# Seven half-size products for the last quarter of one token group's first matrix product, and a new order of work around it

## The chip, the cores and the metric

The kernel runs on one NeuronCore of a Trainium2 chip. Its engines are TensorE (PE, with PEld for its weight loads), VectorE (DVE), ScalarE (ACT), GpSimd (POOL) and SyncE (SP, which here only issues DMAs). The metric is the time of one execution on the device in microseconds. Before the change it is 272.64 us, the median of three runs (272.38 to 273.44).

## What is computed

Linear attention with cosine weights for 8 batches of 8 heads, 576 positions and 64 features, followed by a two-layer network on the 4608 tokens that come out:

```python
r = np.maximum(x, 0.0)                      # x is q or k
phi = np.concatenate([r * cos, r * sin], axis=-1)
kv = np.einsum('bhsf,bhsd->bhfd', k_p, v)
z = np.sum(k_p, axis=2)
num = np.einsum('bhsf,bhfd->bhsd', q_p, kv)
den = np.einsum('bhsf,bhf->bhs', q_p, z)[..., None] + 1e-06
x = (num / den).transpose(0, 2, 1, 3).reshape(4608, 512)
h = x @ w_in                                # 512 x 2048
g = np.maximum(0.01 * h, h)
out = g @ w_out                             # 2048 x 512
```

Inputs and output are float32; the matmuls take float16 and accumulate in float32.

## The kernel before

**Groups.** The tokens are worked in nine groups, numbered 0 to 8, of 512: group b below 8 holds the first 512 positions of batch b, group 8 the last 64 positions of all eight. "Third group" is group 2 and "fourth group" group 3. Each group goes through the same stages: k and v are loaded, k is multiplied with cosine and sine (`k_cos(b,j,engine)`, `k_sin`, nine slices j each, tile `kp`), v is cast (`v_pairs`, tile `vm`), `kv_sum(b)` multiplies them (72 matmuls); q is loaded, multiplied (`q_prep(g,j)`, tile `qp`) and transposed by DMA (`q_transpose_dma`, tile `qpT`); `num(g,j)` makes 128 tokens' numerators and denominators in the one PSUM buffer `ps_num`, and three DVE operations (`den`, `rden`, `xs`) divide them; the four `xs` are transposed, from group 3 on by one DMA (`x_transpose_dma(g)`, tile `xT`). `load(k,b)` and its like issue on SP's queue into four `stage` buffers, so that a load waits until its buffer's last tenant has been read.

**First product.** In groups 0 to 2 `M(g,m)` makes 128 of the 2048 columns of h for all 512 tokens with four matmuls of 512 columns (L634), and ACT applies the leaky ReLU to two m at once (L645, tile `g`). From group 3 on (`F7 = 3`) a quarter u of the columns is made by seven half-size products in Winograd's form: `P(g,u,n)`, n = 1 to 7, is four matmuls of 256 columns (L787). They need sums of quarters of x (`x_sum(g,n,engine)`: X1, X2, X4, and n = 3, which overwrites a quarter of `xT`) and of the weights (`w1_sum(bp,n,engine)`: W1, W2, W4 in `wext`, and n = 3, which overwrites a quarter of the weights). The products of one quarter share three of four PSUM banks `ps_f`, and `e(g,u,letter)` combines them: b copies the first bank to the third, s copies the second to `s5`, u copies the third to `u1`, z and y are DVE additions, and a, c, d, e are leaky ReLUs from PSUM to `g` on ACT (L814). b, s and u run on ACT, with capital letters on DVE. So P6 waits for b, P3 for s, P7 for u, P4 for y, and the next quarter's P5 for a.

**Second product.** From group 1 on it is made by seven half-size products for the whole group: `F(g,i)`, i = 0 to 27, is four matmuls of 256 columns (L904); `g_sum` makes the sums of g on DVE.

**Order.** Nothing is scheduled at run time: a table of operations (`PROGRAM`, 1,126 entries) is walked from the top, and every operation appends its instructions to its engine's queue. Each engine works its own queue in that order and waits on semaphores. The line order of the table is thus the order in each engine's queue, and the engine letter at an operation's end (D, A, P) says whose queue it is.

The lines that the change touches stand below; in `w1_sum` and `x_sum`, `need` is an assertion at build time that an operation has already been recorded, and issues nothing.

Of the kernel before, what the change touches and what calls it, by code (L numbers as in the profile page):

```python
# [54 lines left out]
F(1,13) k_cos(3,1,P) F(1,14) k_sin(3,8,P) k_cos(3,4,A) k_sin(3,3,D) k_cos(3,8,P) F(1,15) v_pairs(3,2,4,P)
q_transpose_dma(3,0) k_cos(3,7,A) q_prep(3,3,0,8,A) k_cos(3,6,D) num(2,2) x_transpose(2,1,A) k_sin(3,7,D)
k_sin(3,2,D) F(1,16) F(1,17) F(1,18) num(2,3) q_transpose_dma(3,1) k_sin(3,1,A) k_sin(3,6,A) F(1,19)
x_transpose(2,2,A) F(1,20) F(1,21) F(1,22) v_pairs(3,0,2,A) x_transpose(2,3,A) F(1,23) kv_sum(3,0,4,n) M(2,0)
load(v,4) w1_sum(0,1,D) M(2,1) num(3,0) M(2,2) M(2,3) w1_sum(1,1,D) num(3,1) load(k,4) M(2,4) M(2,5) M(2,6)
# [10 lines left out]
kv_sum(4,0,4,n) P(3,1,3) F(2,9) P(3,1,7) e(3,1,z) e(3,0,c) e(3,1,e) num(4,0) F(2,10) w1_sum(1,3,D) F(2,11)  # L70
P(3,2,1) F(2,12) P(3,2,5) e(3,2,b) k_cos(5,6,A) e(3,1,y) num(4,1) P(3,2,6) k_cos(5,3,D) P(3,1,4) k_sin(5,1,P)
e(3,2,s) k_sin(5,6,P) k_cos(5,4,P) q_prep(5,0,0,8,P) P(3,2,2) F(2,13) k_sin(5,2,D) num(4,3) F(2,14) P(3,2,3)
e(3,1,c) e(3,2,u) e(3,2,z) e(3,2,a) load(q,6) P(3,2,7) e(3,1,d) e(3,2,y) k_sin(5,5,A) k_cos(5,2,A)
q_prep(5,2,0,8,P) F(2,16) e(3,2,e) k_cos(5,8,A) P(3,3,1) num(4,2) q_prep(5,3,0,8,D) F(2,15) P(3,3,5)
k_cos(5,5,P) q_prep(5,1,0,8,D) F(2,17) e(3,3,b) x_transpose_dma(4) q_transpose_dma(5,0) v_pairs(5,2,4,A)
P(3,3,6) F(2,18) P(3,3,2) g_sum(2,4,0,4) e(3,3,s) e(3,3,u) k_cos(5,7,A) P(3,2,4) e(3,2,c) P(3,3,3)
x_sum(4,1,P) F(2,19) g_sum(2,4,4,8) F(2,20) k_sin(5,4,P) k_cos(5,0,A) v_pairs(5,0,2,A) P(3,3,7) e(3,3,a)
k_sin(5,0,P) e(3,3,y) e(3,3,c) F(2,21) e(3,2,d) F(2,22) e(3,3,z) e(3,3,e) F(2,23) F(2,24) F(2,25) F(2,26)
F(2,27) P(3,3,4) e(3,3,d) P(4,0,1) e(4,0,b) F(3,0) x_sum(4,2,D) P(4,0,5) F(3,1) load(k,6) e(4,0,s) P(4,0,2)
P(4,0,6) F(3,2) x_sum(4,3,D) k_cos(5,1,A) P(4,0,3) k_sin(5,8,A) e(4,0,u) e(4,0,a) g_sum(3,1,4,8,2) P(4,0,7)  # L80
k_sin(5,3,A) k_sin(5,7,P) e(4,0,z) F(3,3) g_sum(3,2,4,8,2) P(4,1,1) g_sum(3,1,0,4,1) e(4,0,e) e(4,0,y)
e(4,1,b) P(4,1,5) g_sum(3,2,0,4,1) kv_sum(5,0,4,n) e(4,1,S) P(4,1,2) e(4,1,a) q_transpose_dma(5,1) P(4,1,6)
e(4,0,c) F(3,4) x_sum(4,4,D) g_sum(3,3,5,8,2) q_prep(6,0,0,8,P) load(v,6) num(5,0) F(3,5) P(4,0,4) e(4,1,u)
P(4,1,3) e(4,0,d) k_cos(6,2,A) P(4,1,7) P(4,2,5) g_sum(3,3,0,4,1) e(4,1,z) k_sin(6,6,P) g_sum(3,3,4,8,2)
# [10 lines left out]
P(5,0,1) e(5,0,b) P(5,0,5) e(5,0,s) F(4,0) P(5,1,1) x_sum(5,2,P) P(5,0,2) q_prep(7,0,0,8,A) F(4,1)
g_sum(4,3,5,8,2) F(4,2) e(5,0,a) g_sum(4,2,0,4,1) x_sum(5,4,D) P(5,0,3) num(6,0) P(5,0,6) e(5,0,u) e(5,0,z)
F(4,3) F(4,4) P(5,0,7) e(5,0,e) e(5,0,y) F(4,5) e(5,1,b) P(5,1,5) e(5,1,s) q_prep(7,2,0,8,D) num(6,1) P(5,0,4)
F(4,6) e(5,0,d) g_sum(4,3,0,4,1) P(5,1,2) e(5,0,c) q_prep(7,1,0,8,P) P(5,1,6) F(4,7) e(5,1,a) P(5,1,3)
e(5,1,u) e(5,1,z) load(v,7) e(5,1,e) P(5,2,1) P(5,1,7) F(4,8) e(5,1,y) e(5,2,b) F(4,9) num(6,2) F(4,10)
# [1125 lines left out]
```

## Time and profile before

| | |
|---|---|
| median of the runs | 272.64 us (272.38 to 273.44) |
| the profiled execution | 272.81 us, its span 271.0 us |
| PE | busy 263.6 us, 97% |
| PEld, DVE, ACT, POOL | 81%, 76%, 66%, 48% |
| granted TensorE clock | 1.0 |

The span runs from the first instruction to the last, and 1.8 us of the execution lie around it. The trace gives for each engine its instructions with their start and duration, and for idle time what ended it. A matmul's duration runs past the start of the next one, as matmuls are pipelined; what a matmul costs is the distance from start to start. For the same reason a row on DVE or ACT may begin a little ahead of the end of the row before.

### The profile page before, as it was taken

How to read it: one execution, taken by the hardware profiler on the slowest of the kernel's cores; microseconds unless marked ns; L12 is line 12 of the kernel's file. 1: busy time of each engine (PE TensorE's matmuls, PEld its weight loads, DVE VectorE, ACT ScalarE, POOL GpSimd, SP SyncE). 2: the span in 40 equal slices, each digit the busy share in tenths (PEclk: the TensorE clock that was granted, in tenths of full speed). 3: DMA queues.
4: the chain of work that ended last, by engine and by line, in shares of the span. 5: the costliest groups of instructions: out<-in, count | busy, mean ns of one | idle time of the engine just before them, and what ended most of it. 6: DMA issues, size and time to landing. Idle time of an engine off the chain costs nothing.

```text
span 271.0 us, 7060 instructions
## 1 busy us (share of the span) xinstructions
PE 263.6 (97%) x2877; PEld 218.5 (81%) x2877; DVE 206.6 (76%) x419; ACT 178.8 (66%) x311; POOL 129.3 (48%) x104
## 2 busy tenths in 40 slices
PE   7899999999999999999999999999999999999993
PEld 3575455656975599999999999999999899999983
DVE  4850597778977897997989689997789967757852
ACT  7856548478966878898788786776834564565500
POOL 2586001992889276979992879743230004000000
PEclk9999999999999999999999999999999999999999
DMA  6999999999999899789959993893565052111214
GB/s 234 359 396 414 379 398 372 373 310 245 293 199 312 182 219 367 239 138 292 300 98 199 252 374 100 141 204 86 120 155 119 2 116 79 41 41 39 80 39 117
DMA packets 75041, 57.07 MB, mean 211 GB/s; under 512 B 47233, under 2 KB 63617, under 8 KB 74625
## 3 DMA queue, kind: packets, MB, share of 16 engines
q1 hardware_dynamic: 74400, 56.11, 74.4%
q10 hardware_dynamic: 608, 0.52, 0.6%
q8 instruction: 22, 0.36, 0.5%
q14 instruction: 11, 0.08, 0.1%
HBM read 36.70 MB, written 9.44 MB: 170 GB/s over the span
## 4 chain that ended last, share of the span: by engine, by line
PE 92%; DMA 3%; POOL 1%; SPq 1%; DVE 1%; issue 0%
PE ps L904 35%; PE ps_f L787 27%; PE ps_h L634 15%; PE ps_o L661 5%; DMA kst<-in_k_dram 3%; PE ps_num L560 3%; PE ps_kv L473 3%; PE ps_f L904 1%; POOL kp L398 1%; PE ps_kv L1004 1%; PE ps_xT L1077 1%; PE ps_qt L546 1%; PE ps_numh L1055 1%; SPq L274 0%; SPq L260 0%; PE ps_x L536 0%
## 5 line engine op out<-in xcount | busy, mean ns | idle before, releaser
L904 PEld LDWEIGHTS <-g 128*128 128x128 f16 x640 | 61.8, 98 | 6.8
L904 PE MATMUL ps<-w,g 128*128 128x256 f16 x496 | 65.1, 273 | 0.0
L814 ACT ACTIVATE g<-ps_f 128x512 f16<-128x512 f32 x72 | 42.0, 598 | 19.1 <-PE ps_f L787 9.7
L634 PE MATMUL ps_h<-xT,w 128*128 128x512 f16 (+1 forms) x208 | 43.5, 363 | 0.0
L787 PEld LDWEIGHTS <-w 128*128 128x128 f16 x384 | 41.6, 114 | 0.7
L787 PE MATMUL ps_f<-xT,w 128*128 128x256 f16 x288 | 42.1, 273 | 0.0
L634 PEld LDWEIGHTS <-w 128*128 128x128 f16 x208 | 22.7, 114 | 16.2
L398 POOL TENSOR_SCALAR kp<-kst,cos_t 128x256 f16<-128x256 f32 (+1 forms) x23 | 30.4, 1328 | 5.0 <-DMA kst<-in_k_dram 5.0
L645 ACT ACTIVATE g<-ps_h 128x1024 f16<-128x1024 f32 x24 | 24.1, 1024 | 12.7 <-PE ps_h L634 12.7
L904 PE MATMUL ps<-T,ext 128*128 128x256 f16 x240 | 32.2, 273 | 0.0
L787 PEld LDWEIGHTS <-wext 128*128 128x128 f16 x288 | 31.3, 114 | 0.6
L904 PEld LDWEIGHTS <-ext 128*128 128x128 f16 x256 | 24.9, 98 | 2.5
L398 POOL TENSOR_SCALAR qp<-qst,cos_t 128x512 f16<-128x512 f32 (+1 forms) x10 | 19.5, 1946 | 9.0 <-DMA qst<-in_q_dram 5.4
L787 PE MATMUL ps_f<-X,wext 128*128 128x256 f16 x144 | 21.5, 273 | 0.0
L687 DVE TENSOR_TENSOR osb<-ps,ext 128x512 f32<-128x512 f32 x23 | 15.8, 687 | 6.4 <-PE ps L904 5.9
L687 DVE TENSOR_TENSOR ps_f<-ps_f,u 128x512 f32<-128x512 f32 x24 | 16.6, 693 | 5.0 <-PE ps_f L787 3.1
L576 DVE TENSOR_TENSOR xs<-ps_num,rden 128x512 f16<-128x512 f32 x28 | 19.4, 691 | 1.0
L398 POOL TENSOR_SCALAR kp<-kst,sin_t 128x256 f16<-128x256 f32 x15 | 18.7, 1249 | 2.3 <-PE ps_kv L473 2.3
L814 ACT ACTIVATE g<-y 128x512 f16<-128x512 f32 x24 | 15.2, 632 | 6.7 <-DVE y L687 6.6
L398 POOL TENSOR_SCALAR qp<-qst,sin_t 128x512 f16<-128x512 f32 (+1 forms) x10 | 19.4, 1942 | 0.0
L687 DVE TENSOR_TENSOR ext<-g 128x512 f16<-128x512 f16 (+1 forms) x24 | 13.9, 578 | 5.1 <-ACT g L645 3.5
L687 DVE TENSOR_TENSOR y<-ps_f,s 128x512 f32<-128x512 f32 x24 | 16.4, 683 | 1.4 <-PE ps_f L787 1.3
(122 smaller groups left out, 457.6 us busy)
## 6 DMA issues: line engine op xcount, KB each, us to landing
out_dram<-osb SPq DMA_DIRECT2D x32, 256.0 KB, 2.9
qst<-in_q_dram SPq DMA_DIRECT2D x7, 1024.0 KB, 9.4
kst<-in_k_dram SPq DMA_DIRECT2D x5, 1152.0 KB, 7.6
vst<-in_v_dram SPq DMA_DIRECT2D x5, 1152.0 KB, 9.8
w2st<-in_moe_w_out_dram SPq DMA_DIRECT2D x3, 1024.0 KB, 12.8
vst<-in_v_dram SPq DMA_DIRECT2D x4, 576.0 KB, 6.7
ext<-in_moe_w_in_dram SPq DMA_DIRECT2D x4, 512.0 KB, 10.5
kst<-in_k_dram SPq DMA_DIRECT2D x2, 576.0 KB, 7.7
```

Of the source, the lines that this page charges most:

```text
L398: eng.tensor_scalar(out=o, in0=i, scalar1=0.0, scalar2=col, op0=ALU.max, op1=ALU.mult)
L473: nc.tensor.matmul(ps[:, o, (c - lo) * NE : (c - lo + 1) * NE], lhsT=st["kp", b][sl, c, j, :], rhs=vm[sl, c, j, :], start=(j == 0), stop=( ...
L546: nc.tensor.transpose(ps[:, h, :], qp[:, h, :], ident)
L560: nc.tensor.matmul(ps[lo:hi, h // 4, (h % 4) * NE : (h % 4 + 1) * NE], lhsT=qpT[:, h, lo:hi], rhs=kv[b][:, h, :],)
L576: nc.vector.tensor_tensor(out=xs, in0=ps[:, :, 0 : 4 * NE].rearrange("p a (b e) -> p a b e", e=NE)[:, :, :, 0:D], in1=rden.rearrange("p (a ...
L634: nc.tensor.matmul(ps[:, m % 2, lo:hi], lhsT=w1[m // 4, c][0][:, w1[m // 4, c][1], m % 4 : 512 : 4], rhs=xT[:, lo // P : hi // P, c, :], s ...
L645: nc.scalar.activation(st["g", g][:, m - 1 : m + 1, :], ps, AF.Lrelu)
L661: nc.tensor.matmul(st["ps_o", g, tt], lhsT=st["g", g][:, m, tt * P : (tt + 1) * P], rhs=w2[:, m, :], start=(m == 0), stop=(m == NFT - 1),)
L687: eng.tensor_tensor(out=o, in0=a, in1=b, op=op)
L787: nc.tensor.matmul(ps[:, mi * HT : (mi + 1) * HT], lhsT=a[:, c, 2 * r0 + mi : 512 : 4], rhs=b[:, c], start=(n in (1, 5) and mi == 0 and c ...
L814: nc.scalar.activation(st["g", g][:, m : m + 2, r * HT : (r + 1) * HT], {"a": A, "c": y22, "e": E, "d": B_}[e].rearrange("p (m t) -> p m t ...
L904: nc.tensor.matmul(ps[:, tt], lhsT=a[:, i, tt * P : (tt + 1) * P], rhs=b[:, i], start=(first and i == 4 * halves[0]), stop=(i == NPR - 1 a ...
```

## The change

A constant `MIX = (3,)` is new: quarter u = 3 of group 2 (m = 10, 11, 14 and 15) is now made by P(2,3,1) to P(2,3,7) and e(2,3,...) in the place of M(2,10), M(2,11), M(2,14) and M(2,15). This brings x_sum(2,1) to x_sum(2,4), asks that all of the weight sums of the second half, W(1,1) to W(1,4), stand before it, and moves the third sum of x (which overwrites a quarter of group 2's `xT`) behind the twelve remaining M(2,m). In the code only the assertions differ:

```diff
+    MIX = (3,)
...
         if n == 3:
-            need(*(("f1", F7 - 1, 8 * bp + 4 + i) for i in range(4)))
+            need(*(("f1", F7 - 1 - (2 * bp + i // 2 in MIX), 8 * bp + 4 + i) for i in range(4)))
...
     def x_sum(g, n, eng):
...
-        if g > F7 and n in (2, 4):
+        if g == F7 - 1 and n == 3:
+            need(*(("f1", g, m) for m in range(NFT) if 2 * (m // 8) + m % 4 // 2 not in MIX))
+        if g >= F7 + (not MIX) and n in (2, 4):
             need(("f1", g - 1, "product", {2: 6, 4: 4}[n]))
```

The rest is the table. From F(1,2) to P(4,0,2) some 200 operations stand in other places, some of them on other engines; behind that three single operations are moved (k_sin(6,5), v_pairs(7,0,2), k_sin(7,2)). Two lines of it:

```diff
-q_prep(4,3,0,8,A) g_sum(2,1,4,6) M(2,12) q_transpose_dma(4,0) q_transpose_dma(4,1) M(2,13) g_sum(2,3,0,6)
...
+q_prep(4,0,0,8,D) M(2,9) M(2,2) M(2,3) F(1,26) x_sum(2,3,D) F(1,25) F(1,24) g_sum(2,1,0,4) P(2,3,1)
+x_transpose_dma(3) k_sin(4,7,D) w1_sum(1,4,D) P(2,3,5) F(2,0) e(2,3,b) x_sum(2,4,P) q_prep(4,2,0,8,P) F(1,27)
```

(Rows of the changed kernel carry line numbers that are 2 to 4 higher: L791 is L787 of before.) On PE there are 16 matmuls of 512 columns fewer and 28 of 256 more. The order of the first product in group 2 is now M(2,6), 7, 0, 1, 12, 13, 4, 5, 8, 9, 2, 3, then P(2,3,...) between F(1,24) to F(1,27) and F(2,0) to F(2,2), and then P(3,0,1). F(2,1), F(2,3) and later ones of F(2,...), which read columns of g that e(2,3,...) writes, stand further back. Three places on the other engines:

**SP, its queue from the loads of group 3 to group 3's x.** Names: `vst`, `kst`, `qst` are loads, `qpT<-qp` and `xT<-xs` DMA transposes, `out_dram<-osb` stores. Before:

```order
L963 DMA out_dram<-osb 128x2x256
L274 DMA vst<-in_v_dram 128x2x576
L510 DMA_TRANSPOSE qpT<-qp 128x16x128 x2
L963 DMA out_dram<-osb 128x2x256 x2
L274 DMA vst<-in_v_dram 128x4x576
L274 DMA kst<-in_k_dram 128x4x576
L524 DMA_TRANSPOSE xT<-xs 128x16x128
L510 DMA_TRANSPOSE qpT<-qp 128x16x128 x2
L274 DMA kst<-in_k_dram 128x4x576
```

With the change:

```order
L967 DMA out_dram<-osb 128x2x256
L512 DMA_TRANSPOSE qpT<-qp 128x16x128
L276 DMA kst<-in_k_dram 128x4x576
L512 DMA_TRANSPOSE qpT<-qp 128x16x128
L276 DMA kst<-in_k_dram 128x4x576
L967 DMA out_dram<-osb 128x2x256
L276 DMA vst<-in_v_dram 128x4x576
L967 DMA out_dram<-osb 128x2x256
L526 DMA_TRANSPOSE xT<-xs 128x16x128
L967 DMA out_dram<-osb 128x2x256
```

The loads of k for groups 4 and 5 and of v for group 4 now stand ahead of group 3's `xT<-xs`, the first two on either side of the second transpose of q; before, the load of k for group 5 stood behind it. The second half of v for group 3 has moved ahead of the four stores that precede these rows.

**DVE, from the fourth division of group 3 (`xs`) to the first sum of group 3's x (`X1b<-xT`).** `wext` and `w_...` are sums of weights, `ext<-g` and `ext<-ext,g` sums of g. Before, the rows behind `xs<-ps_num,rden`:

```order
L687 TENSOR_TENSOR wext<-wext,w_2_0_102 128x1024
L687 TENSOR_TENSOR ext<-g 128x1024
L687 TENSOR_TENSOR wext<-wext,w_0_0_98 128x1024
L687 TENSOR_TENSOR ext<-g 128x512
L687 TENSOR_TENSOR g<-g 128x6x256
L687 TENSOR_TENSOR wext<-w_0_2_99,wext 128x1024
L687 TENSOR_TENSOR ext<-ext,g 128x1024
L687 TENSOR_TENSOR wext<-w_2_2_103,wext 128x1024
L687 TENSOR_TENSOR ext<-ext,g 128x512
L398 TENSOR_SCALAR kp<-kst,cos_t 128x4x64
L398 TENSOR_SCALAR kp<-kst,sin_t 128x4x64
L687 TENSOR_TENSOR X1b<-xT 128x512
```

With the change, from that `xs` on:

```order
L578 TENSOR_TENSOR xs<-ps_num,rden 128x512
L400 TENSOR_SCALAR qp<-qst,cos_t 128x8x64
L400 TENSOR_SCALAR qp<-qst,sin_t 128x8x64
L689 TENSOR_TENSOR xT<-xT 128x2x2x128
L689 TENSOR_TENSOR ext<-g 128x1024
L400 TENSOR_SCALAR kp<-kst,sin_t 128x4x64
L689 TENSOR_TENSOR wext<-w_2_2_103,wext 128x1024
L689 TENSOR_TENSOR osb<-ps_1178,ext 128x512
L689 TENSOR_TENSOR ext<-ext,g 128x1024
L689 TENSOR_TENSOR ps_f_1558<-ps_f_1558,u_184 128x512
L689 TENSOR_TENSOR X1b<-xT 128x512
L689 TENSOR_TENSOR y_186<-ps_f_1559,s_185 128x512
```

Between the division and `X1b` there now stand a `qp` pair, group 2's third sum of x (`xT<-xT`) and the first of group 2's combining additions (`ps_f<-ps_f,u`, which is z); of the four weight sums that stood here one is left (`wext<-w_2_2`, W(1,4)); the others have moved ahead of the division.

**ACT, ahead of kv_sum(4).** `vm<-vst` is the cast of v, `kv<-ps_kv` the copy of kv_sum's result. Before, both casts of group 4's v stood among group 2's leaky ReLUs, more than a dozen rows ahead of `kv_174<-ps_kv`:

```order
L404 CAST vm<-vst 128x18x64
L645 ACTIVATE g<-ps_h 128x1024
L396 ACTIVATE qp<-qst,cos_t 128x8x64
L396 ACTIVATE qp<-qst,sin_t 128x8x64
L645 ACTIVATE g<-ps_h 128x1024
L404 CAST vm<-vst 128x18x64
L645 ACTIVATE g<-ps_h 128x1024
```

With the change:

```order
L818 ACTIVATE g<-y_186 128x2x256
L818 ACTIVATE g<-ps_f_1559 128x2x256
L398 ACTIVATE kp<-kst,sin_t 128x4x64
L818 ACTIVATE g<-ps_f_1557 128x2x256
L406 COPY s_185<-ps_f_1556 128x512
L406 COPY ps_f_1557<-ps_f_1559 128x512
L927 COPY ext<-ps_1572 128x512
L406 CAST vm<-vst 128x18x64
L818 ACTIVATE g<-ps_f_1558 128x2x256
L818 ACTIVATE g<-y_186 128x2x256
L482 CAST kv_174<-ps_kv 128x2x4x66
```

One cast now stands directly ahead of kv_sum(4)'s matmuls, behind the copies s and b of quarter (3,1) and the copy `ext<-ps`; the other is on POOL.

More of the change, by code (lines that the diff above doesn't have):

```diff
@@ L55 @@
[L55 to L59, printed above, removed]
@@ L70 @@
[L70 to L74, printed above, removed]
@@ L75 @@
[L75 to L84, printed above, removed]
@@ L95 @@
[L95 to L99, printed above, removed]
@@ new lines @@
+e(4,0,u) e(4,0,a) g_sum(3,1,4,8,2) P(4,0,7) k_sin(5,3,A) k_sin(5,7,P) e(4,0,z) F(3,3) g_sum(3,2,4,8,2)
+P(4,1,1) g_sum(3,1,0,4,1) e(4,0,e) e(4,0,y) e(4,1,b) P(4,1,5) g_sum(3,2,0,4,1) kv_sum(5,0,4,n) e(4,1,S)
+P(4,1,2) e(4,1,a) q_transpose_dma(5,1) P(4,1,6) e(4,0,c) F(3,4) x_sum(4,4,D) g_sum(3,3,5,8,2)
+q_prep(6,0,0,8,P) load(v,6) num(5,0) F(3,5) P(4,0,4) e(4,1,u) P(4,1,3) e(4,0,d) k_cos(6,2,A) P(4,1,7) P(4,2,5)
+g_sum(3,3,0,4,1) e(4,1,z) k_sin(6,6,P) g_sum(3,3,4,8,2) q_prep(6,1,0,8,D) k_sin(6,1,P) e(4,1,e) F(3,6) F(3,7)
```

104 lines of the change are left out of this document (62 added, 42 removed).

## The prediction

> **What bounds the kernel now.** First the page: who is busy, and whether TensorE's clock was granted.
>
> ```profile
> span 271.0 us, 7060 instructions
> PE 263.6 (97%) x2877; PEld 218.5 (81%) x2877; DVE 206.6 (76%) x419; ACT 178.8 (66%) x311; POOL 129.3 (48%) x104
> PEclk9999999999999999999999999999999999999999
> ```
>
> PE is busy 97% at full clock. Then the busy time in stretches of 10 us where the change lies:
>
> ```profile
> 80.00:90.00 10.00, 10.00 (x75) 5.67 (x74) 6.36 (x15) 6.02 (x8) 9.87 (x5) 1.00 0.94 302
> 90.00:100.00 10.00, 10.00 (x73) 7.52 (x72) 9.17 (x18) 8.34 (x12) 3.12 (x3) 1.00 0.97 176
> 100.00:110.00 10.00, 10.00 (x161) 9.38 (x158) 7.64 (x17) 8.27 (x18) 7.74 (x8) 1.00 1.00 347
> 110.00:120.00 10.00, 10.00 (x111) 9.57 (x110) 9.74 (x22) 9.34 (x18) 10.00 (x5) 1.00 0.72 194
> ```
>
> The columns behind the length are PE, PEld, DVE, ACT, POOL, the clock, the DMA engines' share and GB/s. PE has no idle time here: every wait of PE would be new, and every matmul less is time saved. DVE and ACT are at 60 to 97%, so they can become late. The chain that ended last gives prices per matmul:
>
> ```profile
> 88.45 6.05 PE ps_h L634 x28
> 94.50 2.62 PE ps L904 x24
> 97.11 0.87 PE ps_f L787 x8
> ```
>
> 6.05/28 = 0.216 us for 512 columns, 2.62/24 = 0.109 and 0.87/8 = 0.109 us for 256.
>
> **The change on PE.** Four M go: 16 x 0.216 = 3.46 us. Seven P come: 28 x 0.109 = 3.05 us. Net -0.40 us. All other matmuls are the same in number and only change places.
>
> A rule that speaks against this change stands in the Trainium skill, "TensorE: Matmul & The Clock Gate", section "Back-to-back issue gap": in a stream of weight loads and matmuls a matmul takes about 131 ns at 512 columns and about 81 ns at 128. By it, and an estimate of 98 ns for 256 on the line between, the exchange would cost 28 x 98 - 16 x 131 = +0.65 us. The same section's formula for isolated matmuls gives 216 and 109 ns, and it is this one that the rows above agree with.
>
> **Where PE can wait.** I lay the new order of PE out from the start of group 2's first product, which has the same work ahead of it in both orders:
>
> ```profile
> 79.46 1.92 PE L634 MATMUL ps_h<-xT,w 128*128 128x512 f16 x8
> 81.21 0.42 PE L560 MATMUL ps_num<-kv,qpT 128*128 128x66 f16 x8
> 81.46 1.89 PE L634 MATMUL ps_h<-xT,w 128*128 128x512 f16 x8
> ...
> 96.95 0.60 PE L787 MATMUL ps_f<-xT,w 128*128 128x256 f16 x4
> ...
> 104.91 1.32 PE L473 MATMUL ps_kv<-vm,kp 64*128 64x66 f16 x72
> ```
>
> From start to start a num takes 0.25 us (81.46 - 81.21), an M 4 x 0.216 = 0.864, a P or F 4 x 0.109 = 0.437, and a matmul row of a P ends 0.60 us after its start. Four num, twelve M and three F lead to P(2,3,1): 79.46 + 1.0 + 10.37 + 1.31 = 92.15. Nine P and F further, P(3,0,1) starts at 96.1 (96.95 before). The prices of the others:
>
> ```profile
> 17.28 0.69 DVE L576 TENSOR_TENSOR xs<-ps_numh,rden 128x512 f16<-128x512 f32 x1
> 83.65 0.17 DVE L571 TENSOR_SCALAR den<-ps_num 128x8 f32<-128x8 f32 x1 [0.26 <-PE ps_num L560]
> 84.09 0.69 DVE L576 TENSOR_TENSOR xs<-ps_num,rden 128x512 f16<-128x512 f32 x1
> 84.69 1.22 DVE L687 TENSOR_TENSOR g<-g,ext 128x2048 f16<-128x2048 f16 x1
> 88.92 0.69 DVE L576 TENSOR_TENSOR xs<-ps_num,rden 128x512 f16<-128x512 f32 x1
> 90.94 0.68 DVE L687 TENSOR_TENSOR wext<-wext,w 128x1024 f16<-128x1024 f16 x1
> 95.86 0.35 DVE L398 TENSOR_SCALAR kp<-kst,cos_t 128x256 f16<-128x256 f32 x1
> 96.38 0.42 DVE L687 TENSOR_TENSOR X1b<-xT 128x512 f16<-128x512 f16 x1
> 111.91 0.77 DVE L398 TENSOR_SCALAR kp<-kst,sin_t 128x256 f16<-128x256 f32 x1
> ```
> ```profile
> 18.03 0.40 PE L1077 MATMUL ps_xT<-ident,xs 128*128 128x128 f16 x4 [0.26 <-DVE xs L576]
> ```
> ```profile
> 95.41 1.04 ACT L645 ACTIVATE g<-ps_h 128x1024 f16<-128x1024 f32 x1
> 97.63 0.57 ACT L404 COPY ps_f<-ps_f 128x512 f32<-128x512 f32 x1 [1.19 <-issue]
> 98.11 0.59 ACT L404 COPY s<-ps_f 128x512 f32<-128x512 f32 x1
> 115.76 1.15 ACT L404 CAST vm<-vst 128x1152 f16<-128x1152 f32 x1
> ```
>
> PE resumes 18.03 - 17.97 = 0.06 us after DVE's row ends. DVE passes from `xs` to its next row in 0.60 us (84.09 to 84.69), a division takes 1.04 (83.65 to 84.69), and ACT passes from copy to copy in 0.48.
>
> *Leaky ReLU ahead of P(2,3,1).* Its banks were those of M(2,2) and M(2,3), of which the last ends at 91.0, three F ahead. ACT's 1.04 us and 0.06 end at 92.1, against 92.15: no wait, no slack.
>
> *Short round trips.* b is read by ACT between P1 and P2 of a quarter. For (3,0) only two operations of 0.437 lie between: P1 starts, ends 0.60 later, ACT starts 0.03 to 0.08 after (97.55 to 97.63), 0.57 for the copy and 0.06 make 1.26 to 1.31, against 3 x 0.437 = 1.31. The same holds for a of (3,0) ahead of P(3,1,5). I take 0; from 0 to 0.1 us in all.
>
> *DVE between the fourth division and X1b.* The second division starts at its old place, 83.65, since num(3,1) does. Behind it stand W(0,1), a `kp` row, X2 and W(0,2) (0.65 + 0.3 + 0.35 + 0.65, from the rows above), so the third division starts at 86.65 and ends its `xs` at 87.8, 0.25 us ahead of num(3,3) at 88.0 (0.06 included); then a `kp` row and two weight sums (1.6) and the fourth `xs` is there at 90.4, against 88.92 + 0.69 = 89.61 before. z of the new quarter cannot start before P(2,3,3) ends at 95.4; 0.60 later X1b starts, and with its 0.42 and 0.06 it is there at 96.5, when P(3,0,5) starts at 96.1 + 0.44 = 96.54. Of u(3,0), now on DVE, the same count leaves 0.1 us ahead of P(3,0,7). I take 0.
>
> *Group 3's x.* The transposing DMA leaves SP when the fourth `xs` stands, at 90.4:
>
> ```profile
> 89.64 1.93 SPq L524 DMA_TRANSPOSE xT<-xs  x1
> ...
> 116.02 1.79 SPq L524 DMA_TRANSPOSE xT<-xs  x1
> ```
> ```profile
> 122.07 1.16 POOL L687 TENSOR_TENSOR X<-xT 128x512 f16<-128x512 f16 x1 [1.99 <-DMA xT<-xs]
> ```
> ```profile
> DMA to landing us min/median/max: 4.2/4.7/6.0
> ```
>
> The last row is over the trace's six; the second of those shown took 122.07 - 116.02 = 6.05. With 4.7 it lands at 95.1, 1.0 us ahead of P(3,0,1); with 6.05 at 96.45, and P(3,0,1), then X1b, are 0.4 late. I take 0.05, as the loads that I find ahead of it (below) are through by then or nearly so.
>
> *The cast of v ahead of kv_sum(4).* P(3,0,7) starts at 100.05 and ends at 100.65; y on DVE (0.68), then s, b and `ext<-ps` on ACT (3 x 0.48), then the cast (1.15) and 0.06 end at 104.0; the first matmul of kv_sum(4), 9 operations behind P(3,0,7), starts at 103.97. I take 0.05, from 0 to 0.3.
>
> *Loads.* k for group 4 leaves SP behind the first transpose of q, and DVE's first row on it comes at 85.3 (a division and a weight sum behind 83.65):
>
> ```profile
> 72.75 6.11 SPq L510 DMA_TRANSPOSE qpT<-qp  x2
> ```
> ```profile
> kst<-in_k_dram SPq DMA_DIRECT2D x5, 1152.0 KB, 7.6
> wext<-in_k_dram SPq DMA_DIRECT2D x1, 1152.0 KB, 12.6
> ```
>
> 72.75 + 1.93 for the transpose = 74.7, and 7.6 later, at 82.3, it is there: 3 us of slack. Cost 0. v for group 5 has now k's buffer of group 4 and leaves SP only when the last `kp` row of group 4 is done, near 102; behind it stand q for group 6 and group 4's transpose of x, which is wanted at 114 (116.02 less what the order gains). Its user, the cast of v, stands ahead of kv_sum(5) at 127: cost 0 to a landing of 12.6 us and more.
>
> *The new quarter's other work.* ACT gets three copies and four half-size leaky ReLUs, some 7 x 0.5, for two full ones of 1.04; DVE gets z, y and three x sums, 2 x 0.6 + 3 x 0.35; POOL one x sum. All of it lies beside PE, under the seven P and the F among them; where that cover is thin, the points above have counted it. From P(4,0,2) on the order is the old one; three moved single rows there cost nothing, as each stays far ahead of its user.
>
> **Sum.** -0.40 + 0.05 + 0.05 + 0.05 for the round trips = -0.25 us. The profiled execution, 272.81 us (271.0 and 1.8 around it), lies 0.17 above the median; 272.64 - 0.25 = 272.4 us. 0.5%, or 1.36 us, is about what a measurement of this kernel can tell from no change.
>
> **Rivals.**
> 1. *Waits eat the gain* (still within 0.5%). POOL is busy nearly all through 86 to 97 in the new order, with q_prep(4,2) and five `kp` rows, and DVE's `kp` row took 0.77 us beside a busy POOL (111.91) and 0.35 beside an idle one (95.86). Two `kp` and two `qp` rows behind z and the division, lengthened by 0.4 each, put z's successors 0.4 to 0.8 late, and x's landing adds 0.4. For it: DVE had 97% here at 110 to 120. Against: 1.5 us of DVE's own waiting lie ahead of z. Time 272.64 - 0.40 + 0.8 to 1.2 = 273.0 to 273.5. The Trainium skill, "GPSIMD Engine Reference", section "Key points", says that the two engines share SBUF interfaces and contend in some forms of DVE instruction; by that rule, the two rows agree.
> 2. *Slower: k for group 4 is not there.* DVE stops at its first row on it, the next division waits behind, and PE at num(3,3), since `ps_num` is one buffer. Landing in 12.6 us, as one load of this size did, means 87.3: 2.0 us late, less 0.25 us of slack ahead of num(3,3): +1.75. Time 272.64 - 0.40 + 1.75 = 274.0, and more with a wait for x; it decides from a landing of about 85.5 on. For it: the DMA engines' share is 0.94 and 0.97 of full at 80 to 100. Against: what leaves with it, k for group 5 and v for group 4, leaves behind it, and only one transpose stands close ahead.
> 3. *More than the 0.40 comes off*, 1 us or more: 271.3. PE had no idle time that a better order could win back.
> 4. *The sustained rate of the skill's rule holds*: 272.64 + 0.65 = 273.3; the three chain rows speak against it.
> 5. *The seven P are no shorter than four M*: if weight loads (PEld 9.4 of 10 us busy) set the pace at 114 ns, 28 x 0.114 = 3.19, and 272.5, not to be told from the forecast.
>
> **How the numbers follow.** Forecast (waits of 0 to 0.6 us, with 5): 0.62, 272.1 to 272.9. Rival 1: 0.22. Rival 2, and whatever else makes more than 1.8 us of waits: 0.10. Rival 3: 0.04. Rival 4: 0.02. Faster by over 0.5%: 0.04; slower by over 0.5%: 0.10; the rest, 0.86, within. The range takes in the forecast with 0.2 us for the scatter of the runs at its lower end, and rival 1 with as much at its upper one: 271.9 to 273.7.
>
> **What would show it.** Right: PE still without idle from 80 to 120; P(3,0,1) some 0.85 us and P(4,0,1) some 0.4 us earlier; the P rows at 0.109. Wrong: a wait of PE or PEld on `xT<-xs` or X1b at P(3,0,1) or P(3,0,5), on `vm` at kv_sum(4), or on `xs` at num(3,3) with DVE waiting for `kst` ahead of it. What would make it wrong is a transpose that takes over 6 us behind the earlier loads, or DVE rows that lengthen beside POOL more than these did.

## The result, and the profile after

The changed kernel takes 273.93 us, the median of 13 runs (273.20 to 274.46); the kernel before, run beside it, 272.82 us (13 runs, 272.35 to 273.58). The ratio is 1.0034, 95% interval 1.0023 to 1.0045: 0.93 us slower by the ratio (0.63 to 1.23); the two medians lie 1.11 us apart. The forecast was 0.25 us faster, 272.4, with 273.7 as the range's upper end. The profiled execution took 273.93 us. First its page, the lines that stand in the prediction for the kernel before:

```profile
span 272.1 us, 7097 instructions
PE 263.5 (97%) x2889; PEld 219.6 (81%) x2889; DVE 211.4 (78%) x431; ACT 177.1 (65%) x309; POOL 130.7 (48%) x106
PEclk9999999999999999999999999999999999999999
```

PE's busy time is what it was; the span is 1.1 us longer. Then the busy time by stretches (length, then PE, PEld, DVE, ACT, POOL, the clock, the DMA engines' share, GB/s):

```profile
80.00:90.00 10.00, 10.00 (x75) 5.66 (x74) 9.57 (x23) 6.42 (x9) 6.04 (x5) 1.00 1.05 295
90.00:100.00 10.00, 10.00 (x87) 8.99 (x86) 9.07 (x19) 7.38 (x14) 8.91 (x7) 1.00 1.00 232
100.00:110.00 10.00, 9.10 (x148) 8.22 (x147) 8.24 (x18) 8.26 (x16) 8.05 (x6) 1.00 1.05 263
110.00:120.00 10.00, 10.00 (x111) 9.49 (x110) 8.69 (x20) 7.57 (x14) 10.00 (x8) 1.00 0.66 186
```

PE was busy 10.00 of 10 us in all four stretches before; now 0.9 us of idle time stands between 100 and 110. The timeline of PE there (start, duration, what; in brackets the idle time ahead and what ended it):

```profile
91.10 1.47 PE L908 MATMUL ps<-w,g 128*128 128x256 f16 x12
92.41 0.60 PE L791 MATMUL ps_f<-xT,w 128*128 128x256 f16 x4
...
95.90 1.04 PE L791 MATMUL ps_f<-xT,w 128*128 128x256 f16 x8
96.82 0.63 PE L791 MATMUL ps_f<-X1b,wext 128*128 128x256 f16 x4
97.29 0.60 PE L908 MATMUL ps<-T,ext 128*128 128x256 f16 x4
...
103.43 1.03 PE L908 MATMUL ps<-w,g 128*128 128x256 f16 x8
104.48 1.32 PE L475 MATMUL ps_kv<-vm,kp 64*128 64x66 f16 x72
105.73 1.06 PE L791 MATMUL ps_f<-xT,w 128*128 128x256 f16 x8
107.67 0.43 PE L562 MATMUL ps_num<-kv,qpT 128*128 128x66 f16 x8 [0.88 <-DMA qpT<-qp]
```

The last row is num(4,0). The eight matmuls ahead of it start at 105.73 and take 8 x 0.109, so it could have started at 106.60: PE lost 1.07 us, waiting for group 4's first transposed q. In the stretch from 60 to 135 us the chain of work that ended last leaves PE at this place alone:

```profile
97.89 0.85 PE ps_f L791 x8
98.74 8.89 DMA qpT<-qp
107.63 0.05 issue
107.67 0.43 PE ps_num L562 x8
```

And the queue of SP shows why the transpose left at 98.74:

```profile
90.81 3.05 SPq L526 DMA_TRANSPOSE xT<-xs  x1
95.08 0.38 SPq L967 DMA_DIRECT2D out_dram<-osb  x1
95.57 2.18 SPq L512 DMA_TRANSPOSE qpT<-qp  x1
97.85 0.80 SPq L262 DMA_DIRECT2D qst<-in_q_dram  x1
98.74 6.04 SPq L512 DMA_TRANSPOSE qpT<-qp  x1
```

The row at 95.57 is `q_transpose_dma(4,1)`, that at 97.85 the 1 MB load of q for group 5, and that at 98.74 `q_transpose_dma(4,0)`, the one that num(4,0) and num(4,1) read first. Before, both stood directly behind group 3's x, 15 us ahead of num(4,0), as the same queue of the kernel before shows:

```profile
92.16 4.84 SPq L510 DMA_TRANSPOSE qpT<-qp  x2
```

Between num(2,1), ahead of the change, and kv_sum(5), behind it, lie 57.61 us (71.74 to 129.35); before, 56.63 (71.65 to 128.28). That difference of +0.98 us is made up as follows (a gap is the distance of two starts less the price of the matmuls between them):

| | us |
|---|---|
| matmuls exchanged, by their prices | -0.40 |
| num(4,0) waits for its transpose | +1.07 |
| x_transpose(2,2) at 76.58 waits for DVE's copy of the one ahead | +0.11 |
| kv_sum(4): a gap of 0.18 where it was 0.09 | +0.09 |
| X1b ahead of P(3,0,5): 96.82, where 95.90 + 8 x 0.109 = 96.77 | +0.05 |
| sum | +0.92 |

### The profile page after: what moved, and what is told of

It reads as the page before. It is cut to its first block, busy times and chain, and to the rows that moved or that the text cites. A ratio compares the mean times of both kernels' runs of the same rounds, so it can differ in the third digit from the quotient of the medians.

```text
span 272.1 us, 7097 instructions
## 1 busy us (share of the span) xinstructions
PE 263.5 (97%) x2889; PEld 219.6 (81%) x2889; DVE 211.4 (78%) x431; ACT 177.1 (65%) x309; POOL 130.7 (48%) x106
## 4 chain that ended last, share of the span: by engine, by line
PE 89%; DMA 7%; POOL 1%; SPq 1%; DVE 1%; issue 0%
PE ps L908 34%; PE ps_f L791 27%; PE ps_h L636 14%; PE ps_o L663 5%; DMA qpT<-qp 3%; DMA kst<-in_k_dram 3%; PE ps_num L562 3%; PE ps_kv L475 2%; PE ps_f L908 1%; POOL kp L400 1%; PE ps_kv L1008 1%; PE ps_xT L1081 1%; PE ps_qt L548 1%; PE ps_numh L1059 1%; PE ps_x L538 0%; SPq L276 0%
## 5 line engine op out<-in xcount | busy, mean ns | idle before, releaser
L908 PE MATMUL ps<-w,g 128*128 128x256 f16 x496 | 65.9, 273 | 0.0
L818 ACT ACTIVATE g<-ps_f 128x512 f16<-128x512 f32 x75 | 43.6, 597 | 19.6 <-PE ps_f L791 11.6
L791 PEld LDWEIGHTS <-w 128*128 128x128 f16 x400 | 43.1, 114 | 0.8
L791 PE MATMUL ps_f<-xT,w 128*128 128x256 f16 x300 | 43.4, 273 | 0.0
L636 PE MATMUL ps_h<-xT,w 128*128 128x512 f16 (+1 forms) x192 | 40.1, 361 | 0.0
L791 PEld LDWEIGHTS <-wext 128*128 128x128 f16 x300 | 32.7, 114 | 0.6
L400 POOL TENSOR_SCALAR kp<-kst,cos_t 128x256 f16<-128x256 f32 (+1 forms) x23 | 28.2, 1236 | 6.6 <-DMA kst<-in_k_dram 4.4
L647 ACT ACTIVATE g<-ps_h 128x1024 f16<-128x1024 f32 x22 | 22.1, 1022 | 13.0 <-PE ps_h L636 13.0
L791 PE MATMUL ps_f<-X,wext 128*128 128x256 f16 x152 | 22.7, 273 | 0.0
L400 POOL TENSOR_SCALAR kp<-kst,sin_t 128x256 f16<-128x256 f32 x16 | 20.8, 1304 | 0.0
L406 ACT COPY ps_f<-ps_f 128x512 f32<-128x512 f32 x23 | 13.2, 576 | 7.2 <-PE ps_f L791 6.1
```

The source lines that it names most:

```text
L400: eng.tensor_scalar(out=o, in0=i, scalar1=0.0, scalar2=col, op0=ALU.max, op1=ALU.mult)
L406: nc.scalar.copy(o, i)
L636: nc.tensor.matmul(ps[:, m % 2, lo:hi], lhsT=w1[m // 4, c][0][:, w1[m // 4, c][1], m % 4 : 512 : 4], rhs=xT[:, lo // P : hi // P, c, :], s ...
L647: nc.scalar.activation(st["g", g][:, m - 1 : m + 1, :], ps, AF.Lrelu)
L791: nc.tensor.matmul(ps[:, mi * HT : (mi + 1) * HT], lhsT=a[:, c, 2 * r0 + mi : 512 : 4], rhs=b[:, c], start=(n in (1, 5) and mi == 0 and c ...
L818: nc.scalar.activation(st["g", g][:, m : m + 2, r * HT : (r + 1) * HT], {"a": A, "c": y22, "e": E, "d": B_}[e].rearrange("p (m t) -> p m t ...
```

## Experiments

All edits are of the table of operations. The theory after the comparison above: one DMA transpose, put behind a load, is the loss.

**a1: the transpose early.**

```diff
-... P(3,1,6) q_transpose_dma(4,0) v_pairs(4,2,4,P)
+x_transpose_dma(3) q_transpose_dma(4,0) k_sin(4,7,D) ...
```

> The changed kernel with one entry moved: q_transpose_dma(4,0) directly behind x_transpose_dma(3), ahead of the load of q for group 5. Theory: of the 1.06 us by which the changed kernel's trace lies behind, 1.07 us is one wait, that of num(4,0) for this transpose, which left SP at 98.74 behind the 1 MB load and landed 8.9 us later. It now leaves near 94 and lands by 100, 6 us ahead of its user: num(4,0) starts at 106.6 and not at 107.67, and all of it stays: 1.07 us less than the changed kernel, from 0.1 below to 0.1 above the kernel before. Rival A: the wait passes on. The load of q for group 5 lands some 2 us later, POOL (busy without a break from 105 to 120) gets late with it, and PE stops at kv_sum(5) or num(5,0) near 130: the time stays 0.5 to 1 us above the kernel before. Rival B: num(4,0) is only where PE's advance is given back, and DVE's or ACT's work behind it sets the pace: the first product of quarter (3,2) then waits on ps_f or y near 110, and less than 0.4 us is won.

Measured: ratio to the kernel before 1.0005 (0.9992 to 1.0017), so nearly all of the 0.93 us is gone. num(4,0) starts at 106.57 without a wait and nothing behind it waits in its place. Something else appeared: PE, 0.46 us earlier than before at kv_sum(2) already, stood 0.42 us ahead of P(3,0,1), for group 3's x. The chain:

```profile
90.41 5.85 DMA xT<-xs
96.26 0.04 issue
```

From issue to landing x took 5.85 us, 0.85 more than in the two profiles that stand above.

**a2: the transpose as late, but no load ahead of it.**

```diff
-... e(2,3,a) load(q,5) k_cos(4,7,P) ...
-... q_transpose_dma(4,0) v_pairs(4,2,4,P)
+... q_transpose_dma(4,0) load(q,5) v_pairs(4,2,4,P)
```

> The changed kernel with the load of q for group 5 moved directly behind q_transpose_dma(4,0), which keeps its place in the table. The transpose leaves about 0.8 us earlier (97.9 against 98.74), so it is late in SP's queue as before, but no load stands between the two transposes of q. Theory: what made it late is the 1 MB ahead of it in the DMA queues, about 4 us at the 240 GB/s seen there; without it the transpose lands in about 5 us, at 103, and num(4,0) doesn't wait: 1.07 us less than the changed kernel. Rival: a second transpose behind a first lands in 8 us by itself, since the two share the engines; then it lands at 106 to 106.7, num(4,0) waits 0 to 0.2 us, and 0.9 us is won all the same, but the landing tells the two apart: 5 us against 8.

Measured: 1.0016 (0.9996 to 1.0035), and in a second comparison, on another chip, 1.0006 (0.9991 to 1.0021):

> a2 once more, as the base of the next two on the same chip. In its first runs it lay 0.45 us above the kernel before (interval -0.1 to 0.95), though in its trace kv_sum(5) starts 0.04 us nearer to kv_sum(2) than before. Expected: 0 to 0.6 above. If the x of group 3 lands as late as it did in a1 and a4 (5.8 and 5.9 us from issue, against 5.0 in the kernel before), P(3,0,1) waits 0.1 to 0.5 us for it in the trace.

`q_transpose_dma(4,0)` left at 97.7 and landed in 5.9 us, not in 8.9, and num(4,0) didn't wait. From num(2,1) to kv_sum(5) it took 56.59 and 56.62 us, as long as before. The 5 us of the theory was too little, the 8 of the rival too much: the load ahead had cost the transpose 3.0 us, and leaving behind it 1.0.

**b1 and b2: the cause alone, in the kernel before.** Only `q_transpose_dma(4,0)` is moved: in b1 behind the load of q for group 5, in b2 directly ahead of it.

```diff
-M(2,12) q_transpose_dma(4,0) q_transpose_dma(4,1) M(2,13)
+M(2,12) q_transpose_dma(4,1) M(2,13)
...
-e(3,0,a) load(q,5) x_sum(3,4,D)
+e(3,0,a) load(q,5) q_transpose_dma(4,0) x_sum(3,4,D)        # b1
+e(3,0,a) q_transpose_dma(4,0) load(q,5) x_sum(3,4,D)        # b2
```

> The kernel before with one entry moved: q_transpose_dma(4,0) directly behind the load of q for group 5, as in the changed kernel; nothing else is changed. It makes the supposed cause alone. The load leaves SP at 99.5, so the transpose leaves at 100.0. Theory: behind the load it takes the 8.9 us that it took in the changed kernel, lands at 108.9, and num(4,0), which started at 107.50, stands 1.4 us (0.6 with a landing of 8 us): the time is 0.6 to 1.6 us above the kernel before. Rival: the landing of a transpose doesn't depend on the load ahead of it; in the 4.4 us of this window it lands at 104.4, and the time is that of the kernel before within 0.2 us.

> b1 with the two swapped: in the kernel before, q_transpose_dma(4,0) leaves at the same late moment, 99.5, but directly ahead of the load of q for group 5. In b1, behind that load, it took 9.1 us to land and num(4,0) stood 1.7 us. Theory: the load ahead costs it about 3 to 4.5 us, so here it lands in 4.5 to 6 us, at 104 to 105.5, 2 us ahead of num(4,0), and the time is that of the kernel before (within 0.2 us). Rival: a transpose that leaves at this time takes 9 us whatever is ahead, since stores and loads under way share the engines: then num(4,0) starts at 108.6, and the time is 1.1 us above the kernel before.

Measured: b1 1.0093 (1.0067 to 1.0118), 2.5 us slower; b2 0.9994 (0.9978 to 1.0010), no slower. The chain of b1, then SP's queue of b2 and the time from issue to landing of its last row:

```profile
100.05 9.12 DMA qpT<-qp
109.16 0.05 issue
109.21 0.43 PE ps_num L560 x8
```
```profile
96.81 0.57 SPq L274 DMA_DIRECT2D kst<-in_k_dram  x1
98.86 0.38 SPq L963 DMA_DIRECT2D out_dram<-osb  x1
99.33 5.19 SPq L510 DMA_TRANSPOSE qpT<-qp  x1
```
```profile
DMA to landing us min/median/max: 7.4/7.4/7.4
```

One entry, moved by itself, makes the loss: num(4,0) 1.71 us late (1.4 expected), and the runs somewhat more than the one trace (1.9 us at its end). Two of b1's six runs, 276.38 and 276.40 us, had a mean granted clock of 0.992 where the other four had 0.997 to 1.0; they are part of that difference, and the section on the hardware comes back to them. In b2 the landing was 7.4 us, where 4.5 to 6 were expected; the load of k stood 2.5 us ahead. It reached 106.7, 0.6 us ahead of its user, by luck rather than by the 2 us of the theory.

**The change again, and b3, a longer wait.**

> The changed kernel again, as it is, so that the edits below have it as their base on the same chip. Expected: 0.9 us above the kernel before, and the 1.07 us wait of num(4,0) for its transpose in the trace.

Measured: 1.0054 (1.0032 to 1.0076). Its profiled execution was the slowest of its runs, 276.95 us. The transpose took 10.3 us to land, num(4,0) waited 2.62 us, and then something new. One row of PE's timeline, and the stretches behind it (the clock is the third column from the end):

```profile
109.05 0.43 PE L562 MATMUL ps_num<-kv,qpT 128*128 128x66 f16 x8 [2.44 <-DMA qpT<-qp]
```
```profile
108.00:110.00 2.00, 0.95 (x15) 0.92 (x16) 0.41 (x3) 0.00 (x0) 2.00 (x2) 1.00 1.01 353
110.00:111.00 1.00, 1.00 (x8) 0.74 (x6) 1.00 (x2) 0.98 (x2) 1.00 (x2) 0.55 1.04 398
111.00:112.00 1.00, 1.00 (x7) 0.69 (x6) 1.00 (x3) 1.00 (x3) 1.00 (x2) 0.50 1.07 380
112.00:113.00 1.00, 1.00 (x6) 0.74 (x5) 0.45 (x1) 0.23 (x1) 1.00 (x2) 0.50 1.10 368
113.00:114.00 1.00, 1.00 (x15) 0.81 (x13) 0.00 (x0) 0.19 (x1) 1.00 (x1) 0.74 0.71 224
```

About 1 us behind the wait the granted clock fell to 0.5 for some 3.4 us, which cost 1.66 us more. To see whether this was the wait's doing, b3 makes a longer one: the kernel before with the transpose behind two loads.

```diff
-F(2,4) k_cos(4,6,A) load(v,5) k_cos(4,2,P)
+F(2,4) k_cos(4,6,A) load(v,5) q_transpose_dma(4,0) k_cos(4,2,P)
```

> The kernel before with q_transpose_dma(4,0) behind two loads (q and v for group 5, 2.2 MB) in place of one, so that num(4,0) waits still longer. It leaves near 101 and by b1's 9.1 us plus 3 to 4.5 for the second load lands at 113 to 115: PE stands 5.5 to 7.5 us. Theory one: a wait costs what it lasts: 5.7 to 7.7 us. Theory two, from the changed kernel's second profile, in which PE stood 2.6 us and the granted clock was then 0.5 for 3.4 us (1.7 us lost beside the wait; after the 1.5 us wait of b1 it stayed at 1.0): here too the clock falls, and the time is 1.7 us or more above the wait itself, 7.4 to 9.5 us.

Measured: 1.0234 (1.0203 to 1.0265), 6.4 us slower. The transpose landed in 11.3 us, 112.2 (113 to 115 expected); PE's row, and two of the stretches:

```profile
112.23 0.58 PE L560 MATMUL ps_num<-kv,qpT 128*128 128x66 f16 x8 [4.60 <-DMA qpT<-qp]
```
```profile
113.00:114.00 1.00, 1.00 (x7) 0.72 (x5) 0.93 (x4) 0.00 (x0) 1.00 (x2) 0.50 0.07 16
114.00:115.00 1.00, 1.00 (x7) 0.69 (x6) 1.00 (x2) 0.45 (x1) 1.00 (x1) 0.50 0.00 0
```

num(4,0) was 4.77 us late, and the half clock from 112.2 to 115.6 accounts for the remaining 1.6 us. By the time alone, 6.4 us, either theory could be claimed (it lies in the range of the first, below that of the second); it is the trace that shows the second one's mechanism, with a smaller wait than it assumed.

**a3, a5, a7: the four M back in the changed order.** Three tries at the term of -0.40 alone; the base is a1 for a3 and a2 for the others. The core of the edit, and as comments where each put the M:

```diff
-    MIX = (3,)
+    MIX = ()
-P(2,3,1) ... P(2,3,7), e(2,3,...), x_sum(2,1..4)
+M(2,10) M(2,11) M(2,14) M(2,15)
     # a3: 14 ahead of F(1,26), 15 behind F(1,24), 10 and 11 ahead of F(2,0)
     # a5: 10, 11, 14, X1, X2, 15, then F(1,26) F(2,0) F(1,27)
     # a7: 14, 15, 10, 11 behind F(1,27), then F(2,0)
```

> The changed order with q_transpose_dma(4,0) early as in a1, and the seven products taken out again: M(2,10), M(2,11), M(2,14) and M(2,15) in their place, the four sums of group 2's x and its eight combining steps left out, W(1,3) and W(1,4) behind M(2,15). This measures the term of -0.40 us. Theory: 16 x 0.216 for 28 x 0.109, so 0.40 us more than a1, 0.2 to 0.6 with small waits of either. Rival A: the seven half-size products bring nothing, because weight loads pace them at 0.114 us or because their round trips over ACT and DVE cost PE what they save: within 0.15 us of a1. Rival B: with DVE and ACT freed of the combining work the order around runs without the small waits (0.05 at X1b, 0.18 at kv_sum(4)), and it is no slower than a1.

> a2 with the seven products taken out: M(2,10), M(2,11), M(2,14) and M(2,15) in their place, group 2's sums of x and combining steps left out, F(1,26), F(1,27) and F(2,0) between M(2,15) and group 3's first product, X1b and X2 ahead of the sums that wait for M(2,15)'s leaky ReLU, and W(1,3), W(1,4) behind kv_sum(4). In a3 DVE stood 4.3 us for that leaky ReLU with X1b behind it, so a3 measured this place in DVE's queue and not the products. Theory: 0.40 us more than a2 (16 x 0.216 for 28 x 0.109), less 0.1 to 0.2 for gaps that go with the combining work: kv_sum(5) 61.0 us behind kv_sum(2). Rival: the seven products bring nothing, because what they add on ACT and DVE costs PE as much: 60.7 to 60.8, no slower than a2.

> a5 with the places mended at which PE waited there (1.7 us for a bank that DVE's osb frees, 0.4 for a leaky ReLU): M(2,14) and M(2,15) ahead of M(2,10) and M(2,11), F(1,27) back behind F(1,24). As in a5 the seven products, group 2's sums of x and its combining steps are left out. Theory: 0.40 us more work on PE than a2, and no more waits: kv_sum(5) 61.0 to 61.2 us behind kv_sum(2), and 0.2 to 0.5 us above a2. Rival: 60.7 to 60.8, as a2: the products bring nothing.

Measured: a3 1.0138 (1.0119 to 1.0157), a5 1.0099 (1.0080 to 1.0117), a7 1.0160 (1.0133 to 1.0187). None is the clean comparison that was meant; each time another engine's queue was late. DVE in a3:

```profile
95.26 0.43 DVE L689 TENSOR_TENSOR ext<-g 128x512 f16<-128x512 f16 x1 [4.30 <-ACT g L647]
99.33 0.42 DVE L689 TENSOR_TENSOR X1b<-xT 128x512 f16<-128x512 f16 x1
```

DVE stood for M(2,15)'s leaky ReLU with X1b behind it, and PE 2.32 us for X1b. In a5 PE stood 1.69 us for a bank that DVE's `osb` frees, in a7 2.34 us for x, whose transpose stood behind a store that waited for F(1,27), and then ran at half clock from 100 to about 103.4. Only a5 can be reckoned up, roughly: it needs 2.61 us more than a2 from kv_sum(2) to kv_sum(5); its three waits (1.69, 0.41 and 0.33) are 2.43 of that, and it lacks 0.1 to 0.3 us of a2's small gaps, which leaves 0.3 to 0.5 us for the products, against 0.40. So the term of -0.40 isn't measured by itself. The direct reading is the timeline of the changed kernel: from P(2,3,1) at 92.41 to 95.90 lie eight half-size operations, 0.436 us each and 0.109 a matmul.

**a4, a6, a8, a9: can the 0.25 us be had?**

```diff
 # a4, on a2
-P(3,0,5) x_sum(3,3,D) F(2,4)          v_pairs(4,0,2,A)
+x_sum(3,3,D) F(2,4) P(3,0,5)          v_pairs(4,0,1,A) v_pairs(4,1,2,A)
 # a6, on a4: the load of k for group 5 behind x
+x_transpose_dma(3) load(k,5)
 # a8: a4's edits on the changed kernel; the load where it was, the two transposes exchanged
-F(1,27) q_transpose_dma(4,1) ... load(q,5) ... q_transpose_dma(4,0) v_pairs(4,2,4,P)
+F(1,27) q_transpose_dma(4,0) ... load(q,5) ... q_transpose_dma(4,1) v_pairs(4,2,4,P)
 # a9, on a8: the load of v for group 4 behind x
+x_transpose_dma(3) load(v,4)
```

> a2 (the load of q for group 5 behind q_transpose_dma(4,0)) and two edits for the small gaps that are left: F(2,4) ahead of P(3,0,5), so that X1b has 0.44 us more to its user, and the cast of v for group 4 in two halves, v_pairs(4,0,1,A) and v_pairs(4,1,2,A), so that kv_sum(4) can begin on the first. Theory: PE's gap ahead of X1b (0.10 us in a2) and 0.09 of the 0.18 ahead of kv_sum(4) go; with the wait gone too the time is 0.2 us below the kernel before (272.4 where that is 272.6), which the runs can hardly tell from no change; in the trace kv_sum(5) starts 60.55 us behind kv_sum(2), against 60.73 in a2 and 60.77 in the kernel before. Rival: the gaps move to the next user (P(3,0,2), which waits for the copy b, and num(4,0), which waits for kv), and the distance stays at 60.73.

Measured: 1.0037 (1.0019 to 1.0056). The two small gaps went, as expected, but x landed 5.9 us from issue and P(3,0,1) waited 0.45 us: 56.76 us from num(2,1) to kv_sum(5), no better than a2. That execution, 273.15 us, was the fastest of the twelve; their median lies 1.1 us above the kernel before, and what the others waited for no trace shows.

> a4 (the load of q for group 5 behind q_transpose_dma(4,0), F(2,4) ahead of P(3,0,5), the cast of v in two halves) with the load of k for group 5 moved back behind group 3's x_transpose_dma, where the kernel before has it. Theory: the x transpose lands 5.0 to 6.7 us from issue in the six traces in which 2.3 MB of loads (k for group 5, v for group 4) leave 7 to 8 us ahead of it, and 4.2 to 5.0 in the three of the old order; with one of the two loads behind it, it lands in 4.2 to 5.0 us, near 95.3, and P(3,0,1) doesn't wait: kv_sum(5) starts 60.5 us behind kv_sum(2) (60.77 in the kernel before), and the runs give 0 to 0.3 us below the kernel before. The q transposes come behind the load of k and land near 105, still ahead of num(4,0) at 106.5. Rival A: the landing of x doesn't depend on the loads, and P(3,0,1) waits 0.3 to 0.5 us again: 0.3 to 1 us above the kernel before, as a4. Rival B: the load of k for group 5 now delays the q transposes by its own 3 to 4 us, and num(4,0) waits 0.5 to 1.5 us: as slow as the changed kernel.

Measured: 1.0085 (1.0063 to 1.0106). x landed in 4.3 us and its wait was gone, as the theory had it. But q for group 5, behind the transposes that the load had slowed, came near 109. ACT's queue, and PE's row:

```profile
109.18 0.72 ACT L398 ACTIVATE qp<-qst,cos_t 128x512 f16<-128x512 f32 x1 [1.63 <-DMA qst<-in_q_dram]
...
110.82 0.56 ACT L406 COPY s<-ps_f 128x512 f32<-128x512 f32 x1
```
```profile
111.44 0.60 PE L791 MATMUL ps_f<-xT,wext 128*128 128x256 f16 x4 [1.23 <-ACT s L406]
```

ACT stood for q of the group after, and the copy s, which P(3,2,3) needs, stood behind it: neither rival, a third transfer at its own limit. PE stood 1.39 us there in an execution of 274.27 us, the fastest of its runs (median 275.21).

> The changed kernel with its two transposes of q for group 4 in each other's place: q_transpose_dma(4,0), which num(4,0) and num(4,1) read, ahead of the load of q for group 5, and q_transpose_dma(4,1), which is read 5 us later, behind it; and a4's two small edits (F(2,4) ahead of P(3,0,5), the cast of v in halves). No load is moved, so q for group 5 comes when it does in the changed kernel. Theory: the first transpose lands near 101, the load at 106, the second transpose in 8 to 9 us near 107.7, ahead of num(4,3) at 111.4; nothing waits for any of them. What is left is x: landing in 5.0 to 5.9 us it costs P(3,0,1) 0 to 0.45 us. kv_sum(5) 60.5 to 60.95 us behind kv_sum(2), the time from 0.25 below to 0.3 above the kernel before. Rival: a wait shows up for the second transpose at num(4,3), or on ACT for q for group 5 (as 1.4 us of PE in a6): 0.5 us or more above the kernel before.

Measured: 1.0020 (1.0004 to 1.0036). In its profiled execution x landed in 5.5 us and the second transpose in 8.4, nothing waited for either, and num(2,1) to kv_sum(5) took 56.39 us: 0.24 less than before, about the forecast's figure. Counted from kv_sum(2), as the expectation counts, it is 60.87 us, within its range but 0.10 more than before: PE came to num(2,1) 0.34 us early and stood as long for a division (`xs`) on DVE, a wait that the later origin leaves out. Farther on 0.16 of that is given back (kv_sum(6) to kv_sum(7) takes 34.46 us, where it was 34.30), so the last matmuls start 0.09 us earlier than before (264.80 against 264.89, both from num(2,1) at 71.65). The execution took 272.77 us; the runs lie between 272.66 and 274.06 with a median of 272.99, 0.41 above the kernel before.

> a8 with the load of v for group 4 moved from ahead of group 3's x_transpose_dma to directly behind it. Theory: with 1.15 MB less ahead x lands in 4.2 to 5.0 us, near 95.3, as in a6, and P(3,0,1) doesn't wait; v lands near 98, ahead of POOL's cast at 100; the first transpose of q, behind v, near 102 to 103.5. Then nothing of this stretch waits, kv_sum(5) starts 60.4 to 60.55 us behind kv_sum(2) (60.77 before), and the time is that of the prediction, 0.2 to 0.35 us below the kernel before. Rival: v now sets the pace: its cast, or the transposes of q and q for group 5 behind it, come late, and the time is 0.5 us or more above the kernel before, as in a6.

Measured: 1.0173 (1.0145 to 1.0200). x landed in 4.3 us, but the second transpose of q in 10.1, at 111.0, and ACT's next `qp` row writes the buffer which that transpose reads:

```profile
111.18 0.72 ACT L398 ACTIVATE qp<-qst,cos_t 128x512 f16<-128x512 f32 x1 [3.16 <-DMA qpT<-qp]
```
```profile
113.43 1.01 PE L791 MATMUL ps_f<-xT,wext 128*128 128x256 f16 x4 [2.76 <-ACT s L406]
114.24 1.06 PE L908 MATMUL ps<-T,ext 128*128 128x256 f16 x4
```

Again the copy s stood behind it; PE lost 2.93 us, and the next four matmuls took 0.81 us instead of 0.44, at half clock. No version beats the kernel before: a1 and a2 equal it within their intervals, a8 lies 0.1 to 1.0 us above it.

## Why the prediction was wrong

- *The exchange on PE, -0.40*: right by the prices, not measured by itself. 0.436 us for a half-size operation; the rate of 131 ns and the 114 ns of the rivals did not appear.
- *Leaky ReLU ahead of P(2,3,1), 0*: right: 91.10 + 12 x 0.109 = 92.41.
- *Round trips, 0.05*: nothing, within what was allowed; from 97.29 to 103.43 no operation waits.
- *DVE, X1b and u, 0*: 0.05 us (0.10 in a2), because z, not x, held DVE until 96.36.
- *Group 3's x, 0.05*: the size was right in this execution, the margin wrong. The transpose left at 90.81, not 90.4 (a weight sum ahead of the division took 1.09 us, not 0.68), and landed at 95.9, not 95.1; P(3,0,1) started at 96.34. That the loads ahead "are through by then or nearly so" did not hold: v for group 4 landed at 93.1. With the two loads where the change puts them, 6 to 7.5 us ahead, x lands 5.0 to 6.7 us from issue, in the old order, a6 and a9 in 4.2 to 5.0, and in a1 and a4 that cost 0.42 and 0.45 us.
- *Cast of v, 0.05*: 0.09.
- *Stretch ahead of group 2's first product, taken as the same*: 0.11 us, for a copy that had gone from ACT to DVE behind a `kp` row.
- *k for group 4, and rival 2*: right that DVE didn't wait; the landing at 82.3 is the forecast's figure by luck. The load left 1.0 us later than forecast, since a transpose of q holds SP for 3 us (the row shown, 6.11 for two) and not for the 1.93 of x, and landed in 6.6 us, not 7.6.
- *Slack ahead of num(3,3), 0.25*: by the prediction's own rows 0.16 (88.0 less 87.78 and 0.06), which would make rival 2's price 1.84, not 1.75. Nothing waited there.
- *The step that failed is the list of loads and what stands behind them.* It followed v for group 5 and what comes later ("behind it stand q for group 6 and group 4's transpose of x"), each to its user, and went no further back than v. `q_transpose_dma(4,0)` had been moved as well, from directly behind x to behind the load of q for group 5, and has no term in the sum: it was put at nothing without a reckoning, and it measured 1.07 us. The list of SP's queue ahead of the prediction ends, with the change, one row behind x and so three short of this transpose. Its price stood in the trace of the kernel before. The prediction read the landings of `xT<-xs` alone, 4.2 to 6.0 us, and with those the term would have come out at 0. The same view of `qpT<-qp` ends at 9.9 us, and the transpose that took so long had left directly behind a load of 1.15 MB:

```profile
123.87 0.43 SPq L274 DMA_DIRECT2D kst<-in_k_dram  x1
124.40 5.86 SPq L510 DMA_TRANSPOSE qpT<-qp  x1
```
```profile
DMA to landing us min/median/max: 4.3/5.1/9.9
```

With 9.9 us a transpose that leaves at 98.74 lands at 108.6, and num(4,0), due at 106.6, stands some 2 us: an estimate from these rows and from times of the changed kernel's trace, about twice what came, but not nothing. The prediction's last line names the danger, a transpose of over 6 us behind earlier loads, but its list of waits has x, v and k in it and not `qpT`.

The nearest rival in time was the first (waits eat the gain, 273.0 to 273.5), with DVE late beside a busy POOL as its mechanism. One DVE row did lengthen beside POOL (the weight sum of 1.09 us), but between 86 and 100 us PE waited for DVE 0.05 us only. What stays open is the last 0.2 to 0.6 us: without the wait for q the traces lie from 0.24 below to 0.4 above the old stretch, the runs' medians 0.2 to 0.55 above the kernel before (a1, a2, a8), in a4 1.1. In the profiled executions x's landing makes most of that spread; in those that left no trace it can't be seen.

## What to carry to other kernels

When an order moves, list every DMA by queue and give each one a departure, a landing and a user, transposes and buffer reuse included; the one without a line is where the loss will be. A transpose within the chip's memory isn't a fixed 5 us: close behind loads of 1 MB and more it took 7.4 to 11.3 us here, so take its price from a row that stands as it will stand, and put what PE reads next ahead of the loads that nobody waits for soon. On a PE that is busy without a gap, the 0.40 us of work saved here, 0.15%, were worth less than one such place.
